# Centroid products of both token halves in one step, on the two row halves of the TensorE array

## The chip, the cores and the metric

The kernel runs on one core of one Trainium2 chip. The metric is the device time in microseconds of one execution, as the median over several runs. Engines are named as in the profile: PE is TensorE (PEld its weight loads), DVE is VectorE, ACT is ScalarE, POOL is GpSimd, SP is the engine that issues the DMAs here.

## The reference

Attention restricted by clusters, then a feed-forward layer with a rational activation, then a soft mixture of experts. The change lies in the attention's assignment of queries and keys to centroids:

```
B, H, S, D = 2, 8, 768, 64        # 16 centroids per head
q_assign = argmax(q_n @ c_n.T)     # per token, over the head's 16 centroids
k_assign = argmax(k_n @ c_n.T)
mask = q_assign[:, :, :, None] == k_assign[:, :, None, :]
scores = where(mask, q @ k.T / sqrt(D), -1e9)
attn = softmax(scores)
x = attn @ v                       # then the two later layers
```

## The kernel before

The attention works on pairs: one pair is two heads of one batch, so there are 8 pairs (p = 0 to 7). Queries and keys are loaded transposed, head dimension on the partitions, as tiles of 128 partitions by 768 tokens. The host lays q and k out twice (`twice` in `lay_out`), so partitions 64 to 127 hold a second copy of what partitions 0 to 63 hold. The later split into high and low parts uses this copy; the centroid products use only the first 64 partitions.

For each pair, `prep(p)` makes a list of small steps. `scores(c)` (line 251) multiplies the centroids with one token half c (384 tokens): four products, for the two heads' q and the two heads' k, each into 32 partitions of one PSUM tile from pool `psM`; they lie on four column groups of the array. Each product in full 32-bit floats is two instructions on the engine, so a step is eight. `scaled(c)` (line 256, ACT) divides by the centroid norms into `sc`, `scT(c)` (line 266) transposes on PE, `best` and `first` (DVE) find the maximum, `ohT`, `count` and `masks` build the one-hot rows, `nonhot` (line 309), `alive` (line 322, PE) and `qalive` (line 326, DVE) apply the masks to q, `qsplit` and `ksplit` (POOL) split into parts.

The order of the work is written out by hand. The attention runs in slots, 12 to a pair, n from -10 to 96. `plan` maps a slot to lists of steps per engine; `add(slot, steps)` puts steps in at an offset, and `run(n, ...)` issues them. In each slot the engines get, in this order: the planned ACT, DVE and POOL steps; `a2_mm` (lines 458 and 459, PE) and its exponential `a2_exp` (line 463, ACT); `a2_av` of the slot before (line 472, PE); `a1_exp` of the slot before (line 401, ACT); `a1_mm` (lines 383 and 384, PE), ten slots ahead; its negated maximum `a1_neg` (line 393, DVE); and last the planned PE steps ("P"). Each engine works through its own queue in this order. Slots below 0 also hold dummy products (`idle`, line 510).

Pair 0 is prepared by a list of its own (`first_pair`), pair 1 partly at the opening, pair 2 from slot -4, and pair p + 3 from slot 12p + 8. In the last case `scores(0)` stands in the pair's slot 9 and `scores(1)` in slot 10; `scaled(0)` stands in slot 11. Slots 4 and 10 of each pair also hold `rows` of `stats` (line 437, PE: two transposes of statistics into a `psM` tile), for which POOL makes `stat` (line 432), and slots 5 and 11 hold `place` (line 444, DVE), which reads that tile. Slots 8 to 11 hold the `alive` products of the pair prepared before, one each, and the DVE steps `qalive` that read them come one slot later. Weight decoding (lines 557 to 625) goes through the same plan.

Every small PE result takes a PSUM tile from one pool:

```
psS = actx.enter_context(tc.tile_pool(name="psS", bufs=2, space=PSUM))
psA = actx.enter_context(tc.tile_pool(name="psA", bufs=1, space=PSUM))
psM = actx.enter_context(tc.tile_pool(name="psM", bufs=3, space=PSUM))
```

`psM` has one tag and three buffers of one bank each; `psS` takes four banks and `psA` one, which makes the eight. A tile is given back after its last reader, and a product into a new tile waits until a buffer is free.

Of the kernel before, what the change touches and what calls it, by code (L numbers as in the profile page):

```python
# [8 lines left out]
F32 = mybir.dt.float32  # L9
# [28 lines left out]
def shape_constants():  # L38
    c = np.zeros((128, C_END), np.float32)
    p = np.arange(128)  # L40
    c[p, C_ID + p] = 1.0
    c[:, C_SUM:C_SUM + 128] = p[:, None] % 32 == p[None, :] % 32
    c[0:32, C_SGN] = 1.0
    c[32:64, C_SGN] = -BIG

    for i in range(3):
        c[96 + 6 * i:99 + 6 * i, C_STAT + i] = 1.0
        c[99 + 6 * i:102 + 6 * i, C_STAT + i] = -1.0
    b = np.zeros((128, B_END), np.float32)
    b[p, B_ID + p] = 1.0  # L50

    b[0:16, B_MASK:B_MASK + 128] = 1.0
    b[16:32, B_MASK + 128:B_MASK + 256] = 1.0
    b[0:16, B_MASK + 256:B_MASK + 272] = 1.0
    b[16:32, B_MASK + 272:B_MASK + 288] = 1.0
    for i in range(64):
        b[i, B_ADD + 256 + i] = -1.0 if i < 32 else 1.0
    b[:, B_RANK:B_RANK + 16] = 16.0 - np.arange(16)
    return c, (b.view(np.uint32) >> 16).astype(np.uint16)
# [3 lines left out]
def tile_kernel(ctx, tc, qT, kT, v, cenT, cenP, consts, constsb, ab, w_in, w_out, phi, w1, w2, out, dbg=None):  # L63
    nc = tc.nc
    PE, ACT, DVE, POOL, SP = nc.tensor, nc.scalar, nc.vector, nc.gpsimd, nc.sync

    B, H, _, S = qT.shape
    D = v.shape[4]
    NP = B * H // 2
    HS = S // 2  # L70
# [36 lines left out]
    att = actx.enter_context(tc.tile_pool(name="att", bufs=1, side="right"))  # L107
# [7 lines left out]
    psA = actx.enter_context(tc.tile_pool(name="psA", bufs=1, space=PSUM))  # L115
    psM = actx.enter_context(tc.tile_pool(name="psM", bufs=3, space=PSUM))

    cT = att.tile([64, H, 32], F32, name="cT")
    cP = att.tile([128, H // 2, D], F32, name="cP")
    cb = att.tile([128, B_END], BF16, name="cb")  # L120
    ph = att.tile([128, NCC, NS], F32, name="ph")
# [45 lines left out]
    def m_tile(dt=F32):  # L167
        if dt == BF16:
            return psM.tile([128, 1024], BF16, tag="m", name="mb")
        return psM.tile([128, 512], F32, tag="m", name="mf")  # L170
# [65 lines left out]
    def prep(p):  # L236

        hp = p % (H // 2)
        r = raws.pop(p)
        o = ops[p % NBUF]  # L240
        hold = {}
        order = [r["q", 0], r["q", 1], r["k", 0], r["k", 1]]
# [3 lines left out]
            return hold[tag]  # L246

        def scores(c):
            m = hold["m", c] = m_tile()
            for g, t in enumerate(order):  # L250
                PE.matmul(m[32 * g:32 * g + 32, 0:HS], cT[:, 2 * hp + g % 2, :],
                          t[0:64, c * HS:(c + 1) * HS], start=True, stop=True)

        def scaled(c):
            sc = hold["sc"] if c else tile_(t_p, "sc", [128, S], F32)
# [81 lines left out]
        if p == 0:  # L337
            return first_pair(r, o, locals())
        return [
            (1, "P", lambda: scores(0)),  # L340
            (2, "P", lambda: scores(1)),
            (3, "A", lambda: scaled(0)),
            (3, "P", lambda: scT(0)),
# [348 lines left out]
    for n in range(-LEAD, NSL + 1):  # L692
        p, k = divmod(n, 12)
# [106 lines left out]
    hp, sp, gts, gsl, lps, Ls = {}, {}, {}, {}, {}, {}  # L800
# [219 lines left out]
    for j in range(4):  # L1020
        for k in range(4):
            PE.matmul(ps[32 * k:32 * k + 32, :], uT[:, k, 32 * j:32 * j + 32], W["wo", j][0][:, k * 512:(k + 1) * 512],
                      start=(j == 0), stop=(j == 3))
# [11 lines left out]
    for a in range(2):  # L1035
        pf = [bank(), bank()]
        for c in range(NCC):
            for fh in range(2):
                for e4 in range(4):
# [3 lines left out]
                              start=(c == 0), stop=(c == NCC - 1))  # L1043
# [63 lines left out]
    for c0, cw in COLS:  # L1107
        ne = 256 // cw
        so = bank()
        for e in range(E):  # L1110
            wt = W["w2", e - e % ne, c0][0][:, (e % ne) * 8 * cw:]
            for kk in range(8):
# [3 lines left out]
                          start=(e == 0 and kk < 4), stop=(e == E - 1 and kk >= 4))  # L1116
# [11 lines left out]
def lay_out(inputs):  # L1128
    def twice(x):
        t = x.transpose(0, 1, 3, 2)  # L1130
        return np.concatenate([t, t], axis=2)


    v = inputs["v"]
    B, H, S, D = v.shape
    v = v.reshape(B * H // 2, 2, S // 128, 128, D).transpose(0, 3, 1, 2, 4)
    w_in = np.ascontiguousarray(inputs["moe_w_in"]).view(np.int64)
    w_in = w_in.reshape(w_in.shape[0] // 128, 128, -1, 128).transpose(2, 1, 0, 3)
    w1, w2 = inputs["moe2_w1"], inputs["moe2_w2"]
    E, DM, F = w1.shape  # L1140
    w1 = w1.reshape(E, 2, 2, 128, F).transpose(0, 1, 3, 2, 4).reshape(E, 2, 128, 2 * F)
    w2 = w2.reshape(E, F // 128, 128, DM).transpose(0, 2, 1, 3)
    w2 = np.concatenate([w2[:, :, :, c0:c0 + cw].reshape(E * cw // 256, 256 // cw, 128, -1).transpose(0, 2, 1, 3)
                         .reshape(E * cw // 256, 128, -1) for c0, cw in COLS])

    cent = inputs["centroids"]
    H, C, D = cent.shape
    cT = np.zeros((D, H, 32), cent.dtype)
    cT[:, :, :C] = cent.transpose(2, 0, 1)
    cP = np.zeros((4, 32, H // 2, D), cent.dtype)  # L1150
    for g in range(4):
        cP[g, :C] = cent[g % 2::2].transpose(1, 0, 2)
    cP = cP.reshape(128, H // 2, D)
    ab = np.concatenate([inputs["moe_a"], inputs["moe_b"]])
    consts, constsb = shape_constants()
    return {
        "qT": twice(inputs["q"]),
        "kT": twice(inputs["k"]),
        "v": v,
        "cenT": cT,  # L1160
        "cenP": cP,
        "consts": consts,
        "constsb": constsb,
        "ab": np.broadcast_to(ab, (128, ab.size)),
        "w_in": w_in,
        "w_out": np.ascontiguousarray(inputs["moe_w_out"]).view(np.int64),
        "phi": inputs["moe2_phi"],
        "w1": w1,
        "w2": w2,
    }  # L1170
# [23 lines left out]
```

## Time and profile before

| what | value |
|---|---|
| median of 3 runs | 601.52 us (599.59 to 604.43) |
| profiled execution, its own time | 601.76 us |
| span of its instructions | 600.0 us |
| busy: PE, DVE, ACT, POOL | 94%, 78%, 65%, 62% |
| mean granted PE clock | 0.992 of full speed |
| DMA | 113.78 MB, 190 GB/s |

The span is the time from the first to the last instruction of the profiled execution; the 1.76 us around it are in its own time. Busy shares are of the span. Attention with the weight decoding takes the first 340 us or so, the feed-forward layer runs to about 520, the experts to the end. In the loop of the attention PE is about 95% busy by the profile, but a product's end is modelled, so that isn't the share of its peak.

### The profile page before, as it was taken

Reading aid. Unit: us, or ns where it says so; the run is one execution under the profiler, and the core shown is the slowest. Engines: PE = TensorE matmul, PEld = TensorE weight load, DVE = VectorE, ACT = ScalarE, POOL = GpSimd, SP = SyncE. Lnnn points to the kernel's source line nnn. Section 1 sums busy time; section 2 is a strip of 40 time slices with the busy share of each in tenths; the row PEclk is TensorE's granted clock in tenths of the full one; section 3 lists DMA queues with packets and bytes.
Section 4 is the critical chain, followed back from the end, with each engine's and each line's share of the span. In section 5 each row is a group of like instructions: output and inputs, shape, how many; then the busy total and the mean of one; then the engine's idle time right before and its main releaser. Section 6 shows DMA issues by size and latency. Waiting matters only on the chain.

```text
span 600.0 us, 9999 instructions
## 1 busy us (share of the span) xinstructions
PE 561.5 (94%) x3391; PEld 351.3 (59%) x3394; DVE 468.3 (78%) x821; ACT 392.7 (65%) x713; POOL 374.1 (62%) x483
## 2 busy tenths in 40 slices
PE   8899999999999999999899989999999999889996
PEld 3455555465555655555554667767677757664375
DVE  5789698798887987888983399999899998952034
ACT  3676768678676877777776487787577767730111
POOL 8659898796996979979657456655466535601000
PEclk9999999999999999999999999999999999989998
DMA  8613564344433644134354367666476637369996
GB/s 223 226 43 115 163 195 148 130 148 163 169 125 133 193 142 124 54 136 144 134 170 134 113 218 277 224 220 232 153 251 211 231 136 282 96 259 376 419 418 257
DMA packets 37907, 113.78 MB, mean 190 GB/s; under 512 B 5216, under 2 KB 5664, under 8 KB 33248
## 3 DMA queue, kind: packets, MB, share of 16 engines
q1 hardware_dynamic: 37856, 113.14, 54.0%
q8 instruction: 27, 0.44, 0.3%
q14 instruction: 24, 0.20, 0.1%
HBM read 96.02 MB, written 15.73 MB: 186 GB/s over the span
## 4 chain that ended last, share of the span: by engine, by line
PE 51%; DVE 26%; ACT 8%; issue 7%; POOL 5%; DMA 2%; SPq 0%; DVEq 0%; POOLq 0%; ACTq 0%
DVE neg L393 5%; PE s L383 5%; PE av L472 4%; PE s L458 4%; PE h L809 4%; PE h L812 3%; PE h L810 3%; PE s L384 3%; PE s L459 3%; DVE p L859 3%; PE pb L1114 2%; DVE p L858 2%; PE pb L1042 2%; DVE mh L564 2%; ACT neg L401 2%
## 5 line engine op out<-in xcount | busy, mean ns | idle before, releaser
L393 DVE TENSOR_SCALAR_CACHE_REDUCE neg<-s 128x768 f32<-128x768 f32 x96 | 91.2, 952 | 36.9 <-ACT neg L401 26.0
L463 ACT ACTIVATE e<-s 128x768 f32<-128x768 f32 x96 | 77.5, 807 | 58.7 <-PE s L459 58.6
L401 ACT ACTIVATE neg<-neg,nv 128x768 f32<-128x768 f32 x96 | 89.4, 932 | 9.8 <-DVE neg L393 9.6
L840 POOL TENSOR_SCALAR q<-u,babs 128x512 f32<-128x512 f32 x47 | 40.3, 857 | 76.1 <-ACT u L838 76.1
L383 PE MATMUL s<-k,q 128*128 128x384 f32 x192 | 75.7, 394 | 12.8 <-DVE neg L393 10.0
L472 PE MATMUL av<-e,vt 128*64 128x384 f32 x384 | 83.2, 512 | 0.2 <-ACT e L463 0.2
L809 PE MATMUL h<-xh,w 128*128 128x512 f32 x192 | 80.7, 420 | 0.4 <-DMA w<-w_in 0.4
L383 PEld LDWEIGHTS s<-k,q 128*128 128x128 f32 x192 | 36.3, 189 | 67.9 <-DVE neg L393 27.6
L810 PE MATMUL h<-xl,w 128*128 128x512 f32 x192 | 76.0, 396 | 0.0
L458 PE MATMUL s<-q,k 128*128 128x384 f32 x192 | 73.1, 381 | 0.7 <-DVE neg L393 0.6
L842 POOL TENSOR_TENSOR q<-q,u 128x512 f32<-128x512 f32 x47 | 63.8, 1357 | 3.9
L384 PE MATMUL s<-k,q 80*128 80x384 f32 x192 | 65.2, 340 | 0.0
L459 PE MATMUL s<-q,k 128*128 128x384 f32 x192 | 64.8, 337 | 0.0
L812 PE MATMUL h<-xh,w 128*128 128x512 f32 x192 | 52.7, 396 | 0.0
L579 POOL TENSOR_TENSOR w<-mh,ex 128x512 f32<-128x512 f32 x32 | 44.2, 1382 | 10.7 <-DMA w_out<-w 5.4
L859 DVE SCALAR_TENSOR_TENSOR p<-q,p 128x512 f32<-128x512 f32 (+1 forms) x49 | 48.7, 996 | 0.1
L849 ACT ACTIVATE r<-q,epsc 128x512 f32<-128x512 f32 (+1 forms) x49 | 33.5, 684 | 20.8 <-POOL q L842 20.5
L809 PEld LDWEIGHTS h<-xh,w 128*128 128x128 f32 x192 | 36.2, 189 | 17.4 <-issue 10.9
L838 ACT ACTIVATE u<-h 128x512 f32<-128x512 f32 x47 | 27.8, 591 | 27.7 <-PE h L812 27.7
L458 PEld LDWEIGHTS s<-q,k 128*128 128x128 f32 x192 | 36.1, 188 | 16.2 <-issue 8.1
L841 DVE TENSOR_TENSOR p<-p,h 128x512 f32<-128x512 f32 x47 | 31.8, 678 | 16.9 <-ACT p L839 16.8
L812 PEld LDWEIGHTS h<-xh,w 128*128 128x128 f32 x192 | 36.3, 189 | 8.8
(193 smaller groups left out, 1228.2 us busy)
## 6 DMA issues: line engine op xcount, KB each, us to landing
wt<-w SPq DMA_DIRECT2D x32, 1024.0 KB, 7.8
w<-w_in SPq DMA_DIRECT2D x96, 256.0 KB, 3.1
raw<-w_in SPq DMA_DIRECT2D x16, 512.0 KB, 3.5
raw<-w_out SPq DMA_DIRECT2D x16, 512.0 KB, 3.4
w_in<-w SPq DMA_DIRECT2D x16, 512.0 KB, 2.7
rawk<-kT SPq DMA_DIRECT2D x14, 384.0 KB, 4.0
rawq<-qT SPq DMA_DIRECT2D x14, 384.0 KB, 3.8
w_out<-w SPq DMA_DIRECT2D x16, 256.0 KB, 3.4
```

The source lines that it names most:

```text
L383: PE.matmul(ps[:, c, 0:HS], o["q1"][:, it], o["k1"][:, w], start=True, stop=False)
L384: PE.matmul(ps[:, c, 0:HS], o["q2"][0:80, it], o["k2"][0:80, w], start=False, stop=True)
L393: DVE.tensor_scalar(neg, s1s.pop((p, idx))[:, :, 0:HS], -1.0, None, ALU.mult, ALU.min, accum_out=nvs[p, half][0][:, 0, col:col + 1])
L401: ACT.activation(neg, neg, AF.Exp, scale=-1.0, bias=nv[:, 0, col:col + 1], accum_out=ssum[:, col:col + 1])
L458: PE.matmul(ps[:, h, 0:HS], o["k1"][:, jt], o["q1"][:, w], start=True, stop=False)
L459: PE.matmul(ps[:, h, 0:HS], o["k2"][:, jt], o["q2"][:, w], start=False, stop=True)
L463: ACT.activation(e, s2s.pop((p, k))[:, :, 0:HS], AF.Exp)
L472: PE.matmul(a[64 * h:64 * h + 64, 0:HS], vs[p][:, h, j, :], e[:, h, :], start=(j == 0), stop=(j == 5))
L809: PE.matmul(h, wh[:, c, :], xh[t][:, c, :], start=(c == 0), stop=False)
L810: PE.matmul(h, wh[:, c, :], xl[t][:, c, :], start=False, stop=False)
L812: PE.matmul(h, wl[:, c, :], xh[t][:, c, :], start=False, stop=(c == NCC - 1))
L859: DVE.scalar_tensor_tensor(p[:, w], q[:, w], 2.0, p[:, w], ALU.subtract, ALU.mult)
```

## The change

For pairs 1 to 7 `scores(0)` does nothing any more, and `scores(1)` computes both token halves: the products of half 0 take partitions 0 to 63 of centroids and of q or k, those of half 1 partitions 64 to 127, the second copy. Both halves' PSUM tiles are allocated at the start of that step. The centroids are laid out twice by the host, so their array `cT` has 128 partitions in place of 64. Pair 0, whose q and k arrive half by half, keeps two steps. Nothing else is changed: not the plan, nor the pools.

```diff
-    cT = att.tile([64, H, 32], F32, name="cT")
+    cT = att.tile([128, H, 32], F32, name="cT")
...
         def scores(c):
-            m = hold["m", c] = m_tile()
-            for g, t in enumerate(order):
-                PE.matmul(m[32 * g:32 * g + 32, 0:HS], cT[:, 2 * hp + g % 2, :],
-                          t[0:64, c * HS:(c + 1) * HS], start=True, stop=True)
+            if p == 0:
+                m = hold["m", c] = m_tile()
+                for g, t in enumerate(order):
+                    PE.matmul(m[32 * g:32 * g + 32, 0:HS], cT[0:64, 2 * hp + g % 2, :],
+                              t[0:64, c * HS:(c + 1) * HS], start=True, stop=True)
+            elif c == 1:
+
+                for c2 in range(2):
+                    hold["m", c2] = m_tile()
+                for g, t in enumerate(order):
+                    for c2 in range(2):
+                        r = slice(64 * c2, 64 * c2 + 64)
+                        PE.matmul(hold["m", c2][32 * g:32 * g + 32, 0:HS], cT[r, 2 * hp + g % 2, :],
+                                  t[r, c2 * HS:(c2 + 1) * HS], start=True, stop=True)
...
-    cT = np.zeros((D, H, 32), cent.dtype)
-    cT[:, :, :C] = cent.transpose(2, 0, 1)
+    cT = np.zeros((2 * D, H, 32), cent.dtype)
+    cT[0:D, :, :C] = cT[D:2 * D, :, :C] = cent.transpose(2, 0, 1)
```

## Rows read from the trace of the kernel before

**Rows 1.** The page: busy time of the engines, and the chain by engine.
```profile
PE 561.5 (94%) x3391; PEld 351.3 (59%) x3394; DVE 468.3 (78%) x821; ACT 392.7 (65%) x713; POOL 374.1 (62%) x483
...
PE 51%; DVE 26%; ACT 8%; issue 7%; POOL 5%; DMA 2%; SPq 0%; DVEq 0%; POOLq 0%; ACTq 0%
```

**Rows 2.** Groups by line and shape, PE: busy us, mean ns | idle before.
```profile
L251 PE MATMUL mf<-rawq,cT 64*32 64x384 f32 x64 | 13.9, 502 | 0.5
L251 PE MATMUL mf<-rawk,cT 64*32 64x384 f32 x64 | 13.9, 495 | 0.1
```

**Rows 3.** The chain in order of time, whole span: start us, us, what.
```profile
3.70 4.30 DMA rawk<-kT
...
75.61 0.85 PE mf L251 x8
...
231.15 0.85 PE mf L251 x8
```

**Rows 4.** Timeline, 110 to 111.5 us: start us, us, engine, line, operation.
```profile
110.16 0.33 PE L322 MATMUL mf<-oT,W 64*128 64x384 bf16 x1
...
110.42 0.51 PE L251 MATMUL mf<-rawq,cT 64*32 64x384 f32 x2
...
111.20 0.45 PE L458 MATMUL s<-q,k 128*128 128x384 f32 x1
...
111.23 0.55 DVE L326 SCALAR_TENSOR_TENSOR qa<-rawq,mf 128x384 f32<-128x384 f32 x1
```

**Rows 5.** Timeline, 113.7 to 117 us; in brackets the idle time before, and its releaser.
```profile
113.80 0.28 PE L437 MATMUL mb<-cb,stat 128*32 128x128 bf16 x2
...
114.00 0.96 DVE L393 TENSOR_SCALAR_CACHE_REDUCE neg<-s 128x768 f32<-128x768 f32 x1 [1.41 <-ACT neg L401]
...
114.02 0.33 PE L322 MATMUL mf<-oT,W 64*128 64x384 bf16 x1
...
114.45 0.11 PEld L251 LDWEIGHTS mf<-rawq,cT 64*32 64x32 f32 x2 [0.35 <-ACT sc L256]
...
115.00 1.04 DVE L444 TENSOR_TENSOR q<-mb,cst 32x384 fp32r<-32x384 bf16 x2
...
115.23 0.44 PE L458 MATMUL s<-q,k 128*128 128x384 f32 x1
```

**Rows 6.** The chain in order of time, 109 to 119 us.
```profile
113.93 0.48 ACT sc L256
...
114.46 0.85 PE mf L251 x8
...
118.03 0.96 DVE neg L393 x2
```

**Rows 7.** Line 251: what PE stood idle for before it (us, times).
```profile
  ACT sc L256: 1.7, 5
```

**Rows 8.** The chain in order of time, 35 to 42 us.
```profile
36.44 0.78 PE mf L251 x8
...
38.95 0.78 PE mf L251 x8
```

**Rows 9.** Timeline, 36 to 44 us.
```profile
37.66 0.24 POOL L432 TENSOR_TENSOR stat<-r,stat 128x12 bf16<-128x12 f32 x1
...
38.40 0.28 PE L437 MATMUL mb<-cb,stat 128*32 128x128 bf16 x2
...
38.72 1.04 DVE L444 TENSOR_TENSOR q<-mb,cst 32x384 fp32r<-32x384 bf16 x2 [0.54 <-PE mb L437]
```

**Rows 10.** DMA issues, 0 to 12 us: KB each, median us to landing.
```profile
cT<-cenT SPq DMA_DIRECT2D x1, 64.0 KB, 2.2
```

**Rows 11.** Windows: PE, PEld, DVE, ACT, POOL busy; PE clock, DMA share, GB/s.
```profile
12.00:15.00 3.00, 1.85 (x13) 0.87 (x12) 2.24 (x4) 0.08 (x1) 2.99 (x2) 1.00 1.02 378
...
525.00:530.00 5.00, 3.31 (x11) 2.93 (x12) 3.86 (x10) 2.15 (x5) 0.00 (x0) 0.66 1.01 426
```

**Rows 12.** Timeline of PE, around 14 and 527 us: idle time before.
```profile
14.36 0.52 PE L293 MATMUL mb<-cb,eq 128*64 128x128 bf16 x6 [1.03 <-DVE pres L302]
...
526.69 1.09 PE L870 MATMUL gt<-cst,p 128*128 128x128 f32 x4 [2.89 <-DVE p L859]
```

## The prediction

> **What bounds the kernel now.** I read the page first, for the shares [rows 1]: TensorE is busy 94% of the span and heads the chain of waits with 51%, VectorE follows with 26%. That says only that TensorE's order matters, so I then took the costs of the one line that changes [rows 2] and asked the chain whether it stands there. It does: the second of the two score steps of a pair lies on the chain in all five pairs that are prepared in the steady loop (pairs 3 to 7, one each 39 us; the first and the last are in [rows 3]), and those five stretches are alike to about 0.1 us, so one of them, around 110 to 118 us, can stand for all.
>
> In that stretch slot 9 of the attention loop runs the first score step and slot 10 the second. In slot 9 [rows 4] TensorE goes from the product of `alive` (110.16) to eight score instructions (110.42) and from them straight to the slot's next `a2_mm` (111.20): 0.78 us of TensorE, with nothing waiting in between. In slot 10 [rows 5] the order is the transposes of `stats` (113.80), `alive` (114.02), the score step (114.45), then `a2_mm` of slot 11 (115.23), again 0.78 us for the step. But here the step waits: TensorE's weight load stood 0.35 us until ACT had ended `scaled(0)`. The chain [rows 6] shows the same: ACT's `sc` at 113.93, then the scores at 114.46, and from there to VectorE's `neg` at 118.03. A score product has no use for `sc`. What it waits for is its PSUM tile: pool `psM` has three buffers, and at this point they hold the result of `rows`, that of `alive(0,1)` and that of `scores(0)`; the first to be given back is the last of these, by `scaled(0)`, which is an ACT step of slot 11. This wait is there five times, 1.7 us in all [rows 7]. So the pool is already short by one buffer in slot 10.
>
> **The change part by part.**
>
> First, slot 9 loses its score step. That takes 0.78 us of TensorE from the path, and all that follows moves up with it, to `neg` of slot 10 at the least: VectorE had been idle for 1.41 us before that `neg` [rows 5], so it can begin 0.78 us sooner. (The row puts this `neg` down to ACT's exponential before it; by the code it needs the slot's `a1_mm`. Both move up by the same 0.78 us, since both follow `a2_mm` of slot 10.)
>
> Second, slot 10 now takes two `psM` tiles at once. Counting tiles there: `rows`, `alive(0,1)`, the scores of the first half, the scores of the second: four tiles for three buffers. The first half gets the buffer of `alive(1,0)`, given back by the `qalive` that VectorE ran from 111.23 to 111.78 [rows 4]. The second must wait for the oldest of the others, `rows`, and that one is given back by `place`, the first VectorE step of slot 11. No choice of buffers avoids it: all three tiles ahead are given back by steps of slot 11, `alive(0,1)` by a VectorE step behind `place`, the first scores only after themselves. `place` stands in VectorE's order right behind `neg` of slot 10: it is the row at 115.00, 1.04 us for two instructions [rows 5], ended at 116.04. Moved up by 0.78 it ends at 115.26.
>
> Third, what is queued behind that wait on TensorE is the rest of the score group and then `a2_mm`, `av` and `a1_mm` of slot 11, and for those wait ACT's two exponentials and `neg` of slot 11. From the release to the start of TensorE takes 0.04 us (113.93 plus 0.48 is 114.41 in [rows 6], and the weight load starts at 114.45 in [rows 5]). The group itself I put at 0.78 us, as one step of today, if the two halves of the rows really run side by side. No row of this trace has products on both row halves at once; the nearest are the four column groups of today's step, of which two instructions of 0.5 us each [rows 2] are over within 0.51 us, at 110.42 [rows 4]. The bounds are thus 0.78 and, with the halves one after the other, 1.56 us. I take 0.78, as the row that it is nearest to runs side by side already. So `a2_mm` of slot 11 starts at 115.26 + 0.04 + 0.78 = 116.08, against 115.23 today: 0.85 us later, even with the 0.78 gained in slot 9 counted. From there the chain runs over `a1_mm` to `neg` of slot 11 [rows 6] and on through VectorE, so nothing gives it back. Five pairs: 5 x 0.85 = +4.25 us.
>
> The Trainium skill has, in "TensorEngine Tiling (Array Packing)", section "Restrictions and Gotchas", a warning that speaks against this change: tiles on different rows must write to different PSUM banks, so row tiling raises PSUM pressure. The trace agrees as far as it can, with the 0.35 us that the step waits for a bank already. On the size of the group, "TensorE: Matmul & The Clock Gate", Part 3, has a packed group last as long as one product plus about 4 ns for each further tile; by that estimate four more tiles would add 0.02 us to the 0.78, and no run here shows it.
>
> Fourth, pair 2 is prepared ahead of the loop, in slots -3 and -2, where the chain runs over TensorE too [rows 8]. The step of slot -3 goes (0.78 us again), but `rows` can't follow all the way: POOL's `stat` ends at 37.90, so it starts at about 37.95 instead of 38.40 [rows 9]. `place` follows 0.32 us later as it does now, at 38.27, takes its 1.04 and ends at 39.31. Plus 0.04 and 0.78 is 40.13, against 38.95 + 0.78 = 39.73 today: +0.4 us.
>
> Fifth, pair 1's scores come at about 20 us as two steps back to back, and now as one. There the chain is with ACT and VectorE, not TensorE, and the three buffers are free enough for two tiles: nothing. Pair 0 keeps its form: nothing.
>
> Sixth, the array `cT` doubles, from 64 to 128 KB [rows 10], on SP's queue ahead of the first q and k. Its issue is one instruction as before. The chain begins with a load of k [rows 3], so 64 KB more could delay it by what they take with all DMA engines busy: at the 378 GB/s of a full stretch [rows 11] 0.17 us. Below that, nothing, if the engines have room. I take 0.1.
>
> `scaled(0)` now comes some 2 us later on ACT, ahead of the exponential of slot 11; that exponential needs `a2_mm` of slot 11, which comes behind the scores anyway, and 0.57 us of `scaled` fit between. Cost nothing, as `a2_mm` takes longer; without that cover 0.6 us a pair.
>
> Sum: 4.25 + 0.4 + 0.1 = +4.75 us. The profiled execution took 601.76 us (span 600.0 and 1.76 around it), so 606.5; the median of the three runs is 601.52, 0.24 lower, which makes 606.3. I say 606.5.
>
> **The rivals.**
>
> The wait isn't there, and the change does what it says: 596.3. Then slot 10's group starts behind `alive`, at 114.02 - 0.78 + 0.26 = 113.50, and `a2_mm` at 114.28, 0.95 us earlier than now, since the wait for `scaled(0)` goes too. Five times that and 0.78 of pair 2 is -5.5 us, and the 0.1 of `cT` leaves -5.4. It decides at the moment the second buffer comes free: the step breaks even if that is 0.85 us ahead of my 115.26, and gains below. For it: 27.8 us of score instructions [rows 2] are on an engine that heads the chain. Against it: the wait of today, which only a shortage of buffers explains, and a fourth tile on top. The skill's "Theoretical Speedup" table in the tiling page (two-fold for a contraction of at most 64) would by itself give this result.
>
> The halves do not run side by side: +0.78 in each of the six groups, +4.7, which makes 611.2. For it: no row shows two row halves, and both write to the same PSUM partitions. Against it: what the column groups do.
>
> Part of the delay is given back, by a chain beside the one shown that had slack in the other direction, say a POOL step of `stat` or `qsplit` that now starts in time: 602.5 to 605. Against it: neighbouring pieces of the chain are in-order queues that all move along.
>
> The clock falls in the new wait. TensorE does the first product of the group and then stands still for about 1.1 us. A wait of 1.03 us left the granted clock at 1.00; one of 2.89 us was followed by a stretch at 0.66 on average, that is, some 3.4 us at the lower level of 1.2 GHz [rows 11, 12]. At most 1.7 us lost for each of five waits: 615. The new wait is close to the harmless one.
>
> **How the numbers follow.** Forecast 0.62, halves one after the other 0.14, part given back 0.10, no wait 0.10, clock 0.04. The forecast's own spread is about 605.5 to 608 (a group somewhat over 0.78, `cT` between nothing and 0.17). The range takes in the partial case and the serial halves, 602.5 to 611.3, and leaves out no wait and the clock. A measurement of this kernel tells about 1% from no change, 6 us: slower than 607.5 are the serial halves, the clock and a sixth to a fifth of the forecast, 0.30; faster than 595.5 is about half of the no-wait case, 0.06; the rest, 0.64, lies within.
>
> **What would show it.** In the changed profile the score line's waits should name VectorE's `place` (line 444 of today) and no longer ACT's `sc`, five times in the loop, above 1 us each. Slot 9 should be some 0.78 us shorter, the step from slot 10's `a2_mm` to slot 11's about 5.6 us against 4.03. The score group should take 0.8 us from the release on; 1.5 would mean serial halves. The pairs' period should rise from 38.9 to 39.8 us. Wrong I am if the score line waits for nothing, or if the second half's products start ahead of `place`'s end. The first q and k products should start at most 0.2 us later.

## The result and the profile after

The changed kernel takes 609.04 us (604.78 to 610.51, four runs) against 601.42 us (599.59 to 604.43, four runs) of the kernel before: ratio 1.0108, 95% interval 1.0077 to 1.0139. It is slower by about 1%. The forecast was 606.5, the range 602.5 to 611.3. The time fell inside the range by luck: two errors of opposite sign nearly cancelled, as the traces below show.

The profiled execution took 608.3 us, its span is 606.4 us (600.0 before) and its mean granted clock 0.984 (0.992 before). In the changed kernel all lines behind `scores` lie some ten lower than before: `place` is line 454, `neg` 403, `a2_mm` 468, `ksplit` 270 and 271, and the new step is line 261.

The page of the changed kernel first: busy time, the granted clock in 40 slices, the chain by engine. It answers to [rows 1].

```profile
PE 565.5 (93%) x3391; PEld 353.0 (58%) x3394; DVE 459.7 (76%) x821; ACT 392.8 (65%) x713; POOL 372.8 (61%) x483
...
PEclk9999999899899899999999999999999999989998
...
PE 51%; DVE 23%; ACT 10%; POOL 8%; issue 7%; DMA 1%; POOLq 0%; DVEq 0%; ACTq 0%; SPq 0%
```

Three slices of the attention have an 8 in the clock line. The kernel before has a 9 in all of them:

```profile
PEclk9999999999999999999999999999999999989998
```

VectorE is busy 8.6 us less than before although it does the same 821 instructions. Both are signs of something that the forecast did not have in its sum.

What TensorE stood idle for ahead of the new line (us, times) answers to [rows 7]:

```profile
its engine sat idle before it (us, times) until:
  issue: 10.2, 12
  DVE q L454: 5.6, 6
...
```

ACT's `sc` is gone from the list and VectorE's `place` has come: 5.6 us in six waits, five of them in the loop. (Most of the 10.2 us of `issue` is idle time of the weight loads over the same waits, 1.74 us each.) The timeline of the changed kernel shows one of them, in slots 10 and 11 of pair 3:

```profile
72.08 0.44 PE L468 MATMUL s<-q,k 128*128 128x384 f32 x1
...
75.17 0.83 PE L261 MATMUL mf<-rawq,cT 64*32 64x384 f32 x2
...
75.88 1.04 DVE L454 TENSOR_TENSOR q<-mb,cst 32x384 fp32r<-32x384 bf16 x2
...
77.07 0.52 PE L261 MATMUL mf<-rawq,cT 64*32 64x384 f32 x3 [1.08 <-DVE q L454]
...
77.88 0.44 PE L468 MATMUL s<-q,k 128*128 128x384 f32 x1
```

The first half's first product runs at 75.17, the rest of the group stands until `place` ends (75.88 + 1.04 = 76.92), and 0.15 us later the 14 instructions that are left run in 77.88 - 77.07 = 0.81 us. From `a2_mm` of slot 10 to that of slot 11 it is 5.80 us (4.03 before).

The chain of the changed kernel holds the new step once for each pair from 2 to 6 (and pair 7 at 238.47):

```profile
39.45 0.87 PE mf L261 x14
...
77.07 0.87 PE mf L261 x14
...
116.08 1.27 PE mf L261 x14
...
157.00 1.23 PE mf L261 x14
...
197.49 0.87 PE mf L261 x14
```

From one to the next it is 39.01 us (77.07 to 116.08), then 40.92, 40.49 and 40.98; before, the four periods from 75.61 to 231.15 [rows 3] are 38.89 us each in the mean. So one period costs 0.1 us and three cost 1.6 to 2.1 us. The windows of the changed kernel tell them apart (us; busy time of PE, PEld, DVE, ACT, POOL; granted clock; DMA share; GB/s). Two of pair 3, then five of pair 4:

```profile
76.00:77.00 1.00, 0.00 (x0) 0.00 (x0) 0.93 (x2) 0.00 (x0) 0.92 (x2) 1.00 0.78 315
77.00:78.00 1.00, 0.93 (x15) 0.33 (x16) 0.54 (x2) 0.00 (x0) 0.91 (x3) 1.00 0.52 209
...
115.00:116.00 1.00, 0.01 (x1) 0.00 (x0) 0.94 (x2) 0.00 (x0) 0.92 (x2) 1.00 0.78 315
116.00:117.00 1.00, 0.92 (x14) 0.21 (x14) 0.53 (x2) 0.00 (x0) 0.91 (x3) 0.71 0.52 209
117.00:118.00 1.00, 1.00 (x9) 0.71 (x3) 0.62 (x2) 0.58 (x1) 0.99 (x2) 0.50 0.00 0
...
119.00:120.00 1.00, 1.00 (x4) 0.16 (x4) 0.00 (x0) 0.97 (x2) 0.92 (x2) 0.58 1.04 415
120.00:121.00 1.00, 1.00 (x6) 0.66 (x4) 0.00 (x0) 1.00 (x3) 1.00 (x3) 1.00 0.87 352
```

In pair 3 the wait leaves the clock at full speed. In pair 4 the same wait is followed by some 3.4 us at the lower level (0.50, that is 1.2 of 2.4 GHz). Pairs 5 (0.56 over 157 to 160) and 6 (0.56 over 198 to 201) go like pair 4, pair 7 (1.00 over 239 to 242) like pair 3.

The most useful reading is a table that I made from the starts of `neg`, one for each slot, each in the changed kernel minus before (us). It is a running account of the delay.

| | slot 9 | slot 10 | slot 11 | slot 12 | slot 13 | slot 9 of the next pair |
|---|---|---|---|---|---|---|
| pair 3 | +0.50 | -0.27 | +1.48 | +1.57 | +0.67 | +0.68 |
| pair 4 | +0.68 | -0.10 | +3.19 | +3.68 | +2.80 | +2.79 |
| pair 5 | +2.79 | +2.02 | +5.30 | +6.50 | +5.16 | +4.33 |
| pair 6 | +4.33 | +3.56 | +6.84 | +8.05 | +6.70 | +6.36 |
| pair 7 | +6.36 | +5.59 | +7.34 | +7.44 | +6.54 | +6.5 |

Ahead of the loop there are already +0.60 us of pair 2. Slot 10 gains 0.77 each time, as forecast; slot 11 stands 0.98 later than slot 9 in the two pairs with an even clock. Then comes what was not forecast: between slots 12 and 13 the delay shrinks by 0.9 us (1.57 to 0.67, 7.44 to 6.54; in the other pairs 0.9 to 1.4). What lasts of a pair is +0.18 where the clock held and 1.5 to 2.1 us where it fell. Where it fell, slot 11 stands 2.5 us later than slot 9 in place of 0.98.

Where it shrinks, a row of VectorE has become shorter. The timelines of VectorE and POOL there, in pair 3 of the kernel before:

```profile
83.90 1.83 POOL L261 TENSOR_TENSOR k<-rawk,k 64x768 fp32r<-64x768 f32 x1
...
84.30 0.36 DVE L275 TENSOR_TENSOR eq<-mf,mx 128x192 bf16<-128x192 f32 x1
84.70 1.25 DVE L283 TENSOR_TENSOR eq<-eq,cb 128x384 bf16<-128x384 bf16 x1
...
86.78 0.94 DVE L393 TENSOR_SCALAR_CACHE_REDUCE neg<-s 128x768 f32<-128x768 f32 x1
```

and of the changed kernel:

```profile
84.51 1.87 POOL L271 TENSOR_TENSOR k<-rawk,k 64x768 fp32r<-64x768 f32 x1
84.62 0.94 DVE L403 TENSOR_SCALAR_CACHE_REDUCE neg<-s 128x768 f32<-128x768 f32 x1
...
85.87 0.36 DVE L285 TENSOR_TENSOR eq<-mf,mx 128x192 bf16<-128x192 f32 x1
86.27 0.36 DVE L293 TENSOR_TENSOR eq<-eq,cb 128x384 bf16<-128x384 bf16 x1
...
87.45 0.94 DVE L403 TENSOR_SCALAR_CACHE_REDUCE neg<-s 128x768 f32<-128x768 f32 x1
```

Before, the product of `eq` takes 1.25 us and ends 0.22 us after POOL's subtraction in `ksplit` (84.70 + 1.25 = 85.95, 83.90 + 1.83 = 85.73). Afterwards the same instruction takes 0.36 us: it arrives when the subtraction is nearly over (86.38). Pairs 4 and 7 have the same long row before. In pairs 5 and 6 `eq` is short already, and the row that stands beside the subtraction is the next one, of the weight decoding. The kernel before in pair 5:

```profile
161.77 1.92 POOL L261 TENSOR_TENSOR k<-rawk,k 64x768 fp32r<-64x768 f32 x1
...
161.91 2.33 DVE L570 SCALAR_TENSOR_TENSOR mh<-raw,mh 128x512 f32<-128x512 uint32 x1
```

and the changed kernel, where the clock had fallen and VectorE meets the subtraction one step earlier, ahead of `neg` of slot 12:

```profile
164.38 1.89 POOL L271 TENSOR_TENSOR k<-rawk,k 64x768 fp32r<-64x768 f32 x1
...
164.49 2.06 DVE L574 TENSOR_SCALAR mh<-raw 128x512 int32<-128x512 int32 x1
...
168.62 0.78 DVE L580 SCALAR_TENSOR_TENSOR mh<-raw,mh 128x512 f32<-128x512 uint32 x1
```

Over the whole run `mh<-raw,mh` is busy 5.7 us less (35.3 to 29.6) and `eq` 2.0 less (6.2 to 4.2).

In pair 3 the subtraction itself stands only 0.6 us later than before: POOL's queue was not held by the new wait. From this my theory: the long row is a wait in the dress of a busy engine, VectorE was going to be late there anyway, and most of the new delay fell into that time. It makes two claims: the wait is nearly free because POOL's subtraction is as late, and what costs is the clock after the wait. The main rival was the forecast's own: the 0.85 us of each pair lasts, and the total is its sum.

### The profile page after: what moved, and what is told of

Its sections match the earlier page's. It is cut to its first block, busy times and chain, and to the rows that moved or that the text cites. A ratio compares the mean times of both kernels' runs of the same rounds, so it can differ in the third digit from the quotient of the medians.

```text
span 606.4 us, 9999 instructions
## 1 busy us (share of the span) xinstructions
PE 565.5 (93%) x3391; PEld 353.0 (58%) x3394; DVE 459.7 (76%) x821; ACT 392.8 (65%) x713; POOL 372.8 (61%) x483
## 4 chain that ended last, share of the span: by engine, by line
PE 51%; DVE 23%; ACT 10%; POOL 8%; issue 7%; DMA 1%; POOLq 0%; DVEq 0%; ACTq 0%; SPq 0%
PE av L482 5%; PE s L393 5%; PE s L468 4%; DVE neg L403 4%; PE s L469 3%; PE h L819 3%; PE h L822 3%; PE h L820 3%; PE s L394 3%; DVE p L869 3%; PE pb L1124 2%; ACT neg L411 2%; PE pb L1052 2%; PE warm L961 2%; DVE p L868 2%
## 5 line engine op out<-in xcount | busy, mean ns | idle before, releaser
L482 PE MATMUL av<-e,vt 128*64 128x384 f32 x384 | 84.8, 521 | 0.2 <-ACT e L473 0.2
L468 PE MATMUL s<-q,k 128*128 128x384 f32 x192 | 74.4, 388 | 0.7 <-DVE neg L403 0.5
L469 PE MATMUL s<-q,k 128*128 128x384 f32 x192 | 65.9, 343 | 0.0
L589 POOL TENSOR_TENSOR w<-mh,ex 128x512 f32<-128x512 f32 x32 | 42.7, 1334 | 11.4 <-DMA w_out<-w 5.4
```

Of the source, the lines that this page charges most:

```text
L468: PE.matmul(ps[:, h, 0:HS], o["k1"][:, jt], o["q1"][:, w], start=True, stop=False)
L469: PE.matmul(ps[:, h, 0:HS], o["k2"][:, jt], o["q2"][:, w], start=False, stop=True)
L482: PE.matmul(a[64 * h:64 * h + 64, 0:HS], vs[p][:, h, j, :], e[:, h, :], start=(j == 0), stop=(j == 5))
```

## The experiments

Each was timed beside the kernel before on the same chip; the ratios are to that.

| label | median, us | ratio, 95% interval | clock of the profile |
|---|---|---|---|
| e1_fill | 603.20 | 1.0022 [1.0001, 1.0043] | 0.993 |
| e2_one_row_half | 609.68 | 1.0114 [1.0086, 1.0142] | 0.981 |
| e3_slot9 | 605.22 | 1.0047 [1.0028, 1.0065] | 0.984 |
| e4_before_scaled | 603.61 | 1.0001 [0.9978, 1.0025] | 0.986 |
| e5_slot9_kcopy | 599.83 | 0.9959 [0.9925, 0.9993] | 0.996 |
| e6_slot9_kcopy2 | 599.05 | 0.9950 [0.9923, 0.9978] | 0.990 |
| e7_before_kcopy | 596.82 | 0.9912 [0.9882, 0.9942] | 0.996 |
| e8_fill_kcopy | 607.03 | 1.0060 [1.0038, 1.0082] | 0.998 |
| e9_before_nosub | 597.61 | 0.9895 [0.9860, 0.9929] | 0.990 |
| e10_fill_nosub | 602.59 | 1.0001 [0.9978, 1.0024] | 0.993 |
| e11_before_kcopy2 | 597.32 | 0.9905 [0.9870, 0.9939] | 0.989 |

**The clock: e1_fill.** The changed kernel, with five products that nothing reads ahead of the group, so that TensorE works in most of the wait.

```diff
                 for c2 in range(2):
                     hold["m", c2] = m_tile()
+                if p > 1:
+                    for _ in range(5):
+                        PE.matmul(hold["m", 0], identb, cb[:, B_MASK:B_MASK + 512], start=True, stop=True)
```

> The changed kernel with five dummy products (bf16, 512 columns, into the first score tile, overwritten after) ahead of each score group of pairs 2 to 7, so that TensorE works in the wait for place. The wait itself stays as long as it is. Theory A: the wait alone costs little in the end, since POOL's queue and the VectorE steps that run beside it take most of the delay back by slot 13 (+0.2 us a pair, +0.6 for pair 2), and the rest of the loss is the TensorE clock that falls to its lower level in the wait of some pairs (+1.5 to 2 us each time). Then the clock stays at 1.00 through the loop and the time is about 603 us (602 to 604). Rival B, the wait itself costs 0.85 us a pair as predicted and the clock is beside the point: no better than 606. Rival C, TensorE's products compete with something and dummies make it worse: over 609.

Measured: 603.20 us, 1.0022. The timeline of e1_fill in the stretch of pair 3 shows the five products, and the group still waiting for `place`, which there is line 457 (75.71 + 1.04 = 76.75); the group starts at 76.92:

```profile
75.00 1.25 PE L260 MATMUL mf<-cb 128*128 128x512 bf16 x5
...
75.71 1.04 DVE L457 TENSOR_TENSOR q<-mb,cst 32x384 fp32r<-32x384 bf16 x2
...
76.92 0.53 PE L264 MATMUL mf<-rawk,cT 64*32 64x384 f32 x4
...
77.70 0.44 PE L471 MATMUL s<-q,k 128*128 128x384 f32 x1
```

The windows of e1_fill behind pair 4's wait are at 1.00, as is each stretch of 50 us from 100 to 250. The delay in slot 11 is still there: from slot 9 to slot 11 the account of `neg` goes from 0.33 to 1.32 in pair 3 and from 0.53 to 1.51 in pair 4, +0.99 and +0.98, as in the changed kernel. But from pair to pair the account goes 0.33, 0.53, 0.74, 0.84, 0.87, 1.06: 0.2 us of a pair remain at most. So the wait by itself costs 1.3 us by the ratio (0.1 to 2.6 by its interval), and most of the 1% is the clock behind it. At an equal mean clock (0.996) it is 1.1 to 2.1 us: three runs of e1_fill took 602.0 to 602.7 us, two of the kernel before 600.6 and 600.9. Both claims of the theory hold so far; a lasting 0.85 a pair would have shown as 4 us here.

**The row halves: e2_one_row_half.** The changed kernel, both halves from partitions 0 to 63, one half's products after the other's.

```diff
-                for g, t in enumerate(order):
-                    for c2 in range(2):
-                        r = slice(64 * c2, 64 * c2 + 64)
+                for c2 in range(2):
+                    for g, t in enumerate(order):
+                        r = slice(0, 64)
```

> The changed kernel with both token halves still in slot 10 and with the same two tiles, but on rows 0 to 63 only, the whole first half ahead of the second. The first half then runs during the wait, the second behind it, 0.78 us as when the two run side by side. Theory A (the place in the order and the two tiles make the loss, the row halves add nothing and cost nothing): as the changed kernel, 605 to 610 us, the score line waiting for place as before. Rival D (products on both row halves at once cost something of their own, in PSUM or in a change of the array's mode): 2 us or more below the changed kernel.

Measured: 609.68 us, 1.0114, not to be told from the change. The timeline of e2_one_row_half has two groups in place of one:

```profile
74.73 0.51 PE L261 MATMUL mf<-rawq,cT 64*32 64x384 f32 x2
...
76.36 0.51 PE L261 MATMUL mf<-rawq,cT 64*32 64x384 f32 x2 [0.78 <-ACT sc L266]
...
77.14 0.44 PE L468 MATMUL s<-q,k 128*128 128x384 f32 x1
```

The second half alone takes 77.14 - 76.36 = 0.78 us; in the changed kernel both halves take 0.81. That shows the row halves of the changed kernel side by side. But it buys nothing here: with the first half done early, its reader `scaled(0)` gives its buffer back (row of ACT, 75.72 for 0.58) before `place` has ended, and the second half takes that one. In the changed order, with the halves alternating, it can't. The edit thus changed two things, the row halves and which buffer is waited for. Slot 11 moves by 0.69 instead of 0.98 in pair 3. The clock fell behind these shorter waits too, of 0.78 us, and in four pairs: it is 0.72 over 115 to 121 us in pair 4, 0.74 over as long a stretch in pairs 5 to 7, and 1.00 in pair 3.

**Without the fourth tile: e3_slot9 and e4_before_scaled.** e3_slot9 is the changed kernel with the merged step one slot earlier, where `rows` holds no buffer, and `scaled` one slot earlier as well; e4_before_scaled has only the earlier `scaled(0)`, in the kernel before.

```diff
-            elif c == 1:
+            elif c == 0:
...
-            (3, "A", lambda: scaled(0)),
+            (2, "A", lambda: scaled(0)),
...
-            (4, "A", lambda: scaled(1)),
+            (3, "A", lambda: scaled(1)),
```

> Both halves side by side in one step as in the change, but in slot 9, where VectorE has already given two tiles back, and scaled(0) and scaled(1) a slot earlier each (slots 10 and 11), so that the tiles come free before slot 10's TensorE steps need them. No wait for place and no fall of the clock in the loop. If TensorE's queue alone set the time, a pair would gain 0.78 of the group and 0.25 of the old wait, 5 us in all: 596.5 us. Theory A (POOL's queue is the hidden second bound of slots 9 to 13 and VectorE falls in step with it at slot 12) gives most of that back: 599 to 601.5 us, with POOL's ksplit at about the same times as in the kernel before.

> The kernel before with nothing but scaled(0) one slot earlier (slot 10 instead of 11), which takes away the 0.25 to 0.35 us that TensorE waits for its tile in slot 10. TensorE's queue alone: five times 0.25, 600.2 us. Theory A (POOL's queue takes it back): 601 to 601.7 us, no difference.

Measured: e3_slot9 605.22 us, slower than before by 0.5%; e4_before_scaled 603.61, no difference within about 1.5 us. In e3_slot9 the wait for a buffer is gone: the group of 16 instructions runs without a stop from 73.04 to `a2_mm` at 73.85, 0.81 us once more. TensorE does get ahead: `neg` moves from +1.49 in slot 10 to +0.10 in slot 12 (e4_before_scaled: from 1.43 to 0.56; both had lost over 1 us earlier, to the clock at the opening or in pair 2's slots). And in slots 13 and 14 it is given back, to +1.18 and +1.56 (e4_before_scaled: 1.05 and 1.42). Here the theory works in the other direction. The timeline of e3_slot9:

```profile
85.67 1.82 POOL L271 TENSOR_TENSOR k<-rawk,k 64x768 fp32r<-64x768 f32 x1
...
85.71 2.33 DVE L580 SCALAR_TENSOR_TENSOR mh<-raw,mh 128x512 f32<-128x512 uint32 x1
```

VectorE now comes to this step of the weight decoding at the very start of POOL's subtraction, and takes 2.33 us for what takes 0.99 at the same place of the changed kernel (86.54). I had expected a gain from e3_slot9 and was wrong by the same step that failed in the prediction: TensorE's gain was booked as lasting. The loss is the clock's once more, in other places: at an equal mean clock (0.990) two runs of e3_slot9 took 603.4 and 604.1 us and four of the kernel before 603.4 to 603.7. In the profiled execution it fell after a wait of TensorE of 1.17 us at 61 us (0.60 in the window from 63, then 0.50) and one of 1.54 us at 89 us.

**POOL's queue shortened: e5 to e8 and e11.** If POOL's subtraction is as late as TensorE, then the copy ahead of it in `ksplit(0)` (0.83 to 0.89 us on POOL) is worth its time. The edit gives that copy to ACT for pairs 3 to 7; in the kernel before ACT is idle for 0.94 us there.

```diff
         def ksplit(h):
...
-            POOL.tensor_scalar(k1, rk, 1.0, 1.0, ALU.mult, ALU.mult)
+            if p < 3 or h not in (0,):
+                POOL.tensor_scalar(k1, rk, 1.0, 1.0, ALU.mult, ALU.mult)
...
+        def kcopy(h):
+            ACT.copy(o[h]["k1"], r["k", h])
...
-        ]
+        ] + ([(4 + 3 * h, "A", lambda h=h: kcopy(h)) for h in (0,)] if p > 2 else [])
```

e5_slot9_kcopy is e3_slot9 with it, e7_before_kcopy the kernel before with it, e8_fill_kcopy is e1_fill with it. e6_slot9_kcopy2 and e11_before_kcopy2 give the copy of `ksplit(1)` to ACT too (`for h in (0, 1)`), on e3_slot9 and on the kernel before.

> The version with both halves in slot 9 and scaled a slot earlier, and from pair 3 on the first copy of ksplit(0) (0.8 to 0.9 us of POOL) made by ACT at the start of slot 12 instead of by POOL, so that POOL's subtraction of ksplit(0) ends that much earlier. Theory A (VectorE is held until that subtraction ends, and so gives back what TensorE gains): neg of slot 13 comes 0.7 to 0.9 us earlier a pair than in the version without this, TensorE's wait ahead of it shrinks and the clock stays up: 597 to 600 us. Rival (POOL has nothing to do with it): as the version without it, 604 to 606 us.

> The same with the copy of ksplit(1) on ACT too, in slot 15. Theory A: POOL's unbroken stretch gets 0.9 us shorter again, but in slot 15 TensorE is the bound, so little is added: 596 to 600 us. If ACT is too full there, 1 us more than the version with one copy.

> The kernel before with the copy of ksplit(0) on ACT from pair 3 on, and nothing else. Theory A: in slots 9 to 11 TensorE's queue and in 12 and 13 POOL's are about equally late, so freeing POOL brings up to 0.7 us a pair: 598.5 to 601.5 us. Rival (POOL has slack): no gain, or a loss by the 0.8 us that ACT gets in slot 12.

> The changed kernel with the five dummy products and the copy of ksplit(0) on ACT from pair 3 on. It is to be held against the kernel before with that copy on ACT. Theory A: with POOL's queue shortened the delay of 0.98 us that the wait for place brings in slot 11 is no longer given back in slot 13, or less of it: 0.5 to 0.9 us a pair, 2.5 to 5 us over the kernel before with the copy on ACT, where without that copy it is 0.2 us a pair. Rival (the delay is given back by something else): again 0.2 us a pair, 1.5 us in all.

> The kernel before with both copies of ksplit on ACT from pair 3 on (slots 12 and 15). The version with one copy on ACT took 0.991 of the time of before. Theory A: in slot 15 the loop is bound by TensorE, so the second copy brings nothing, 596 to 598 us; it would bring 0.5 us a pair, 594, if POOL were the bound there too, and cost as much if ACT were.

Measured: the copy alone, in the kernel before, gives 596.82 us, 0.9912, the lowest median of all and a larger gain than the 598.5 to 601.5 expected. Its account goes -0.23, -0.93, -1.83, -2.81, -3.65, -4.35: some 0.8 us a pair, about the length of the copy. The timeline of e7_before_kcopy, in pair 4, shows the product of `eq` (1.25 us at 123.54 in the kernel before) short, as the subtraction is over 0.11 us after its start:

```profile
120.82 1.89 POOL L262 TENSOR_TENSOR k<-rawk,k 64x768 fp32r<-64x768 f32 x1
...
122.60 0.36 DVE L287 TENSOR_TENSOR eq<-eq,cb 128x384 bf16<-128x384 bf16 x1
```

It isn't this row in every pair: in pairs 3, 6 and 7 of e7_before_kcopy `eq` still takes 1.25 to 1.26 us beside the subtraction, but both stand that much earlier (in pair 3 the subtraction by 0.93, `eq` by 0.94 us, where VectorE has gained in a step ahead, `mh<-raw`, 0.74 us for 1.22). That POOL's queue sets the pace there, in the kernel before, is thus shown from two sides: shortening it gains time, and a delay of VectorE ahead of it is swallowed. The second copy adds nothing (e11_before_kcopy2 597.32, e6_slot9_kcopy2 against e5_slot9_kcopy 599.05 to 599.83; the intervals of their ratios overlap almost wholly). And the row tiling is not worth its place even without the fourth tile: e5_slot9_kcopy, 599.83, is not ahead of e7_before_kcopy, and its account falls by 0.70 us a pair against 0.82.

e8_fill_kcopy went wrong. With POOL ahead, the wait of the change should have cost 2.5 to 5 us against e7_before_kcopy; it cost 607.03 - 596.82 = 10.2. The clock is not it (0.998). In its trace POOL's subtraction, now earlier, meets another VectorE step, the one ahead of `neg` of slot 12: the row `mh<-raw` takes 2.05 us (83.44, pair 3) where the changed kernel has 1.05 in that pair (and 2.06 in pairs 4 to 6, behind the falls of the clock), and ACT has a late `sc`, the copy and an exponential in a row. Which of the two costs how much I did not separate. So moving POOL's work moves the meeting and is no clean test of the theory; the 10 us stay unexplained in part.

**The subtraction left out: e9_before_nosub and e10_fill_nosub.** A cleaner test: leave out the subtraction in the kernel before, and in e1_fill. (That takes its time out of POOL's queue as well as its hold on VectorE; these runs don't tell the two apart.)

```diff
-            POOL.tensor_tensor(k2[0:64, :], rk[0:64, :], k1[0:64, :].bitcast(F32), ALU.subtract)
+            if p < 3 or h:
+                POOL.tensor_tensor(k2[0:64, :], rk[0:64, :], k1[0:64, :].bitcast(F32), ALU.subtract)
```

> The kernel before with the subtraction of ksplit(0) (1.8 us of POOL in slot 12 or 13) left out from pair 3 on, so that the low part of one head's k is that of an older pair; all else is done. Theory A (VectorE's bit and bf16 steps of slots 12 and 13 stand until that subtraction ends): the steps first, bits and mant of those slots go back to 0.4, 0.4 to 0.5 and 0.7 to 0.9 us, and a pair gets 0.7 to 1 us shorter: 596 to 598.5 us. Rival (they are long for another reason): 601 to 602.

> The changed kernel with the five dummy products and with the same subtraction left out. It is to be held against the kernel before without that subtraction. Theory A: nothing in slots 12 and 13 holds VectorE any more, so the delay that the wait for place makes in slot 11 stays, 0.85 to 1.0 us a pair: 4.5 to 5.6 us over it (pair 2's 0.4 to 0.6 counted). Rival (something else gives the delay back): 1 to 2 us over it. Rival (the ten us between the two versions with the copy on ACT were due to the dummies or to the wait itself and not to where the subtraction met VectorE): 8 us or more over it.

Measured: 597.61 against 602.59 us, a difference of 5.0 for the same wait that costs 1.3 with the subtraction in place (e1_fill, 603.20 against 601.9 by its ratio). The accounts, taken from each other (e10_fill_nosub minus e9_before_nosub, at slot 9 of the pairs and behind the last): -0.67, +0.50, +1.38, +2.56, +3.47, +5.05. That is 1.1 us a pair, where e1_fill minus before has at most 0.2. (It starts below 0 because e9_before_nosub had lost over 1 us ahead of the loop, where its clock was 0.66 from 30 to 35 us.) Seen the other way, leaving the subtraction out takes 1% off the kernel before (0.9895), and 0.2% off e1_fill (1.0022 to 1.0001, inside their intervals): there it was hidden behind the wait. The timeline of e9_before_nosub in pair 3 has `eq`, 1.25 us in the kernel before, unhindered without the change:

```profile
85.30 0.36 DVE L284 TENSOR_TENSOR eq<-eq,cb 128x384 bf16<-128x384 bf16 x1
...
85.57 0.99 DVE L571 SCALAR_TENSOR_TENSOR mh<-raw,mh 128x512 f32<-128x512 uint32 x1
```

So with POOL's subtraction out of the way the delay lasts, somewhat larger than the forecast's 0.85 and near the 0.98 of slot 11. The theory stands: it was the subtraction that swallowed it.

## Why the prediction was right, and where it was wrong

**Slot 9** loses 0.78 us: 0.77 measured (slot 10's `neg` from +0.50 to -0.27). Right.

**The count of tiles**, four for three buffers, and the second half waiting for `place`: right, in all five pairs and in pair 2. The argument that no choice of buffers avoids it holds for the order of products that the change has; e2_one_row_half shows that with one half after the other the first half's own buffer does come back first. The warning that I took from the Trainium skill ("TensorEngine Tiling (Array Packing)", section "Restrictions and Gotchas", on PSUM pressure) was borne out: the wait for a bank went from 0.35 to 1.08 us.

**The group**: 0.78 taken, bounds 0.78 and 1.56; measured 0.81, in the changed kernel and in e3_slot9. Side by side, so the rival of serial halves is out. The estimate from the Trainium skill ("TensorE: Matmul & The Clock Gate", Part 3), 0.80, is as near as these rows can tell. From the end of `place` to the first product it is 0.15 us (0.12 to its weight load, at 77.04, which is what the forecast's 0.04 was for ACT's `sc`). Together 0.14 us, which explains the delay of slot 11, +0.98 for +0.85.

**Pair 2**: +0.60 for +0.4, with the same 0.14 in it. **Pair 1**: nothing, right. **`scaled(0)`**: it stands 3 us later and costs nothing, right; the exponential behind it still waits 0.32 us for TensorE. **`cT`**: the first `neg` starts within 0.1 us of before; 0.1 forecast, nothing seen.

**"So nothing gives it back", 5 x 0.85 = +4.25 us: this step failed.** Of 0.98 a pair some 0.8 is given back by slot 13, and five pairs by themselves come to 0.73 us (e1_fill, from 0.33 at slot 9 of pair 3 to 1.06 behind pair 7). I followed the chain from `neg` on "through VectorE" and took each of its rows for work. The rival that had this case, part given back, stood at 0.10, put down against the argument that in-order queues all move along. They don't: POOL's `ksplit` moved only by 0.6 when VectorE moved by 1.57. The rows that would have warned were in the trace: the same `eq` product lasts from 0.357 to 1.249 us, median 0.683, over its eight executions in the kernel before, and `mh<-raw,mh` from 0.68 to 2.33 over its 32. The one stretch taken to stand for all five, 110 to 118 us, ends with slot 11, ahead of these rows, and there the pairs aren't alike.

**The clock: its chance mis-sized.** The rival was held to at most 1.7 us for each of five waits, with a chance of 0.04, because the wait of 1.03 us [rows 12] had left the clock at 1.00 [rows 11]. It fell behind three of five waits, all five of 1.07 or 1.08 us, and a period with a fall cost 1.6 to 2.1 us against 0.1 without: 1.5 to 2.0 more for 1.7 at most. The size was about right, the chance wrong: one harmless row is no bound. By the account at `neg`: +0.50 at slot 9 of pair 3, then 0.18, 2.11, 1.54, 2.03 and 0.18 make +6.5 us behind pair 7, and the span is 6.4 us longer.

So the forecast missed 3.5 us that were given back (5 x 0.85 less 0.73) and some 5 us of clock that came instead; that the two nearly cancel, and the time lies within 3 us of 606.5, is luck. What stays open: why the clock fell in pairs 4 to 6 and not in 3 and 7, with waits of one length, and in e2_one_row_half behind waits of 0.78 us in four pairs of five. One run of the changed kernel had a mean clock of 0.992 and took 604.78 us, so it also differs from run to run.

## What to carry to other kernels

Before merging two steps, count the live tiles of their pool in that slot, and see who gives the next one back. A delay or gain of one engine lasts only if no other queue is as late: look for rows on the chain whose duration varies between executions of the same instruction, since they may be waits; here the best edit was not on the engine that headed the chain but one copy taken from POOL. And a wait of about 1 us on a busy TensorE (0.78 to 1.54 here) can cost more by the clock behind it than by its own length; if it can't be removed, products that nothing reads can hold the clock.

## What the runs showed of the hardware

VectorE's steps of some forms last until a POOL instruction beside them has ended, and the profile counts that time as busy: the product of two bf16 tiles in SBUF 1.25 us for 0.36, the decoding's `mh<-raw,mh` 2.33 for 0.99 and its `mh<-raw` 2.06 for 1.05. The `eq` row ends 0.22 to 0.25 us behind the subtraction's end, in the kernel before, in the changed one (pair 3) and in pair 4 of e7_before_kcopy. Steps that read PSUM are not touched: beside the same subtraction (84.51 to 86.38 in the changed kernel) `neg` takes 0.94 and `eq<-mf,mx` 0.36, as elsewhere. The Trainium skill has this, in "SBUF — State Buffer", section "SBUF: two separate sides": VectorE and GpSimd share one pair of ports as an exclusive lock, which a VectorE step with two SBUF inputs (beside a GpSimd step that reads SBUF) or in a two-port mode needs for its whole length. The rows of `eq` and `mh<-raw,mh`, with two inputs in SBUF, agree with it, and so does e9_before_nosub, in which `eq` takes 0.36 us once the subtraction is gone.

The granted clock falls after the wait, not in it: in pair 4 TensorE stands still at 115 to 116 at 1.00, and the lower level comes with the work from 116 on (0.71, then 0.50).
